# A ConvNeXt V2 block in two passes: set-up and its loads put in another order, and the GRN total placed ahead of the last expansions

## The chip, the cores and the metric

The kernel runs on one core of a Trainium2 chip. The metric is the device time in microseconds (us) of one execution. Profiles are taken by the hardware profiler in one execution of the program; times in them count from the start of the span. The engines are PE (TensorE; its weight loads are listed apart as PEld), DVE (VectorE), ACT (ScalarE), POOL (GpSimd) and SP (SyncE, which here only issues DMAs). ACT and POOL issue some DMAs too.

## The reference

```python
# x: (1, 512, 512, 96) bf16, dw: (3, 3, 96), w1: (96, 384), w2: (384, 96), gamma, beta: (384)
out = depthwise 3x3 convolution of x with dw, zero padding
h = layernorm(out) over the 96 channels            # eps 1e-5
h = gelu_tanh(h @ w1)                              # 384 channels
gx = sqrt((h * h).sum(over all pixels) + 1e-6)     # one value per channel
nx = gx / (gx.mean(over channels) + 1e-6)
h = gamma * (h * nx) + beta + h
return x + h @ w2
```

The global response normalisation (GRN) needs the sum of squares over all 262,144 pixels before any output pixel can be made.

## The kernel before

The image is cut into 128 blocks of 4 rows (2,048 pixels). There are two passes over the blocks.

The first pass is a software pipeline. A loop over slots `s` (L730) issues in each slot the steps that a table `at` has put there, for several blocks at once. For a block `b` the steps are these. `load_x` (L180) brings the block into one of four `xin` tiles, on SP. `turn_x` (L396) transposes it on DVE so that channels lie on partitions, into one of five tiles `xT`. `conv_taps` (L417) makes the depthwise convolution as 72 small matmuls with the weights `Wq`; it needs `xT` of the block and of both neighbours. In even slots without MLP work, and in all MLP slots, its result `Y` lies in one three-bank PSUM tile (pool `psY`, one buffer), in the other slots in banks of the MLP's pools. ACT copies it to `y_bf` and squares it to `ysq`. `stage_stats` sums both with matmuls into `SG`. For the first four blocks (the ramp) `stage_chain` (L518) makes the reciprocal standard deviation on DVE, and `stage_spread` (L544) spreads it by matmuls and an ACT copy to `rbc`; later blocks go by POOL and by DRAM. `stage_norm` (L589) multiplies `y_bf` by `rbc` to `yn` on POOL. `yn` goes to DRAM and comes back as `ynT` with channels on 96 partitions; the other 32 partitions of the six `ynT` tiles stay zero. `mlp_units` (L619) multiplies by the centred weight `w1p` into `U`, takes the gelu on ACT (`gsh`, `gm`), and collects the sums of squares: `bn_stats` on DVE, and a Gram matrix on PE (`gram`). A quarter of the gelu values goes to DRAM for the second pass. Block 0 has its MLP in slot 5.

Between the passes the two last blocks (`RES = 2`) are expanded anew in part (`recompute_units`, six units), two more units of the third block follow (`advance(LEAD, PRE)`), and a chain of short DVE operations makes the GRN scale: `m2`, `ssq`, three Newton steps, `gx` with its row sum `rs_`, then a PE matmul with ones (`tot_ps`), `den`, `gg`, `rden`, `sc`, the scaled weight `W2s` and the bias `B2c`.

The second pass takes the blocks in the order `ORDER`: it loads the kept quarter (`gl`), `ynT` and `x` (`xr`) five blocks ahead, recomputes the other three quarters of the gelu (`gr`), multiplies by `W2s` into `O`, and DVE adds `xb`, which is `x` plus the bias, made by POOL two blocks ahead in one of three buffers.

Every engine runs its instructions in the order in which the program issues them (class `InOrder`, L22). DMA completions are counted on a small set of semaphores that are used in turn.

The set-up stands ahead of the loop. It loads `dw`, x blocks 0 and 1, then the weights on ACT's queue, then x blocks 2 and 3. `Wq` is cleared by POOL and the zero rows of `ynT` are written by DMAs from a zero tile:

```python
pool.memset(Wq[:], 0.0)                                   # L216
for t in yn_ring:
    pool.dma_start(out=t[C:128, :, :], in_=zrow[C:128, None, :].to_broadcast([128 - C, GR, W]))
```

The tap weights `Wd` are made from `dw` by three PE matmuls and DVE, and copied into place in `Wq` by 12 copies (L363 to L370), six on DVE and six on POOL. `busy(n)` (L348) issues `n` matmuls on zeros; `FILL` gives how many, ahead of the tap weights and ahead of the loop. `setup_stats` (L372) clears `SG` and makes `rowsel`; `setup_mlp` (L378) makes `w1p` and the bias through a `psY` tile after slot 1.

Of the kernel before, what the change touches and what calls it, by code (L numbers as in the profile page):

```python
# [16 lines left out]
FILL = (6, 24)  # L17
# [36 lines left out]
def kernel(  # L54
# [105 lines left out]
    with ExitStack() as p1:  # L160
# [45 lines left out]
        for i in range(NI):  # L206
            act.dma_start(out=w1_raw[i:C:NI, :], in_=w1[chans(i), :])
        act.dma_start(out=w2_sb[:], in_=w2.rearrange("(j p) c -> p j c", p=128))
        with nc.allow_non_contiguous_dma("tiny gamma/beta load"):
            act.dma_start(out=gam_bf[:], in_=grn_gamma.rearrange("(j p) -> p j", p=128))  # L210
            act.dma_start(out=bet_bf[:], in_=grn_beta.rearrange("(j p) -> p j", p=128))
        act.activation(out=warm[:], in_=warm[:], func=ACTF.Gelu_apprx_tanh)
        for b in range(2, min(4, NBLK)):
            load_x(b)
        make_identity(nc, ident_f[:])
        pool.memset(Wq[:], 0.0)  # L216
        for t in yn_ring:
            pool.dma_start(out=t[C:128, :, :], in_=zrow[C:128, None, :].to_broadcast([128 - C, GR, W]))
# [5 lines left out]
        dve.memset(cen[:], 1.0)  # L224
# [127 lines left out]

        busy(FILL[0])
# [9 lines left out]
        for h in range(2):  # L363
            for j in range(GR):
                for q in (2 * h, 2 * h + 1):
                    a = q + GR * shift(h, j) - j + 1
                    if 0 <= a < 3:
                        n += 1
                        (dve if n % 2 else pool).tensor_copy(out=Wq[32 * q:32 * q + 32, :, :, j, :],
                                        in_=Wd[32 * q:32 * q + 32, :, 3 * a:3 * a + 3, :])  # L370

        def setup_stats():  # L372
            dve.memset(SG[:], 0.0)
            dve.memset(rowsel[:], 0.0)
            for j in range(GR):
                dve.memset(rowsel[32 * j:32 * j + 32, j:j + 1], 1.0)

        def setup_mlp():  # L378
            dve.memset(w1p[C:128, :], 0.0)
            Us = psY.tile([128, NI, W], f32, name="Y")  # L380
            w1m, b2_ps = Us[:, 0, :E], Us[:, 1, :C]
# [207 lines left out]
        def stage_norm(b):  # L589
# [3 lines left out]
            pool.tensor_tensor(out=yn[:], in0=ybf.pop(b)[:],  # L593
# [134 lines left out]
        setup_stats()  # L728
        store = None
        for s in range(last_slot + 1):  # L730
# [24 lines left out]
            def spread_out():  # L755
                for k in get("spread"):
                    stage_spread(k)
                for b in get("norma"):
                    stage_norm(b)
# [3 lines left out]
            if not mlp:  # L763
                for f in taps:
# [7 lines left out]
                if s + 2 < NBLK:  # L772
                    turn_x(s + 2)
# [57 lines left out]
            if s == 1:  # L831
# [18 lines left out]
        if store:  # L850
            store()
        for j in range(NCH):
# [4 lines left out]
        for n in range(RES):  # L857
            for f in recompute_units(ORDER[n]):
                f()
        made[0] = RES * UPB  # L860
    with p2:
        late.psU2 = p2.enter_context(tc.tile_pool(name="psU2", bufs=2, space=bass.MemoryType.PSUM))
        dve2, pe2, psO = dve, pe, late.psO
        advance(LEAD, PRE)
        gsm = p2.enter_context(tc.tile_pool(name="gsm", bufs=1))
        m2 = gsm.tile([128, NCH, NACC], f32, name="m2")
        dve2.tensor_tensor(out=m2[:], in0=mv[:, :, :, 0], in1=mv[:, :, :, 0], op=ALU.mult)
        dve2.tensor_tensor(out=m2[:], in0=m2[:], in1=mv[:, :, :, 1], op=ALU.add)
        dve2.tensor_tensor(out=m2[:], in0=m2[:], in1=npx[:, None, :].to_broadcast([128, NCH, NACC]), op=ALU.mult)
        ssq = gsm.tile([128, NCH], f32, name="ssq")  # L870
        dve2.tensor_reduce(out=ssq[:], in_=m2[:], axis=AX.X, op=ALU.add)
# [82 lines left out]
```

## Time and profile before

| | us |
|---|---|
| median of 3 runs | 1526.28 |
| range of these runs | 1525.06 to 1527.35 |
| the profiled execution | 1523.96 |
| its span in the profile | 1522.2 |
| busy in the span: ACT | 1448.8 |
| busy in the span: PE | 1424.1 |
| busy in the span: POOL | 1316.3 |
| busy in the span: DVE | 1197.0 |

The first pass takes about the first 977 us of the span, the second the rest. "Busy" counts the instructions of an engine without its register, branch, semaphore and DMA-issuing instructions. The granted clock is the share of full speed that the chip gave PE. A row of the timeline gives the start, the length, the engine, the operation with its output and inputs, how many were merged in the row, and in brackets how long the engine stood idle before it and what it waited for. "Issue" stands for a wait that the profile doesn't show.

### The profile page before, as it was taken

What the parts mean: (1) busy time and instruction counts of PE and PEld (TensorE: products, weight loads), DVE (VectorE), ACT (ScalarE), POOL (GpSimd) and SP (SyncE); (2) the same over time, 40 slices, a digit from 0 to 9 for tenths busy, and PEclk for the clock granted to TensorE, in tenths of its full rate; (3) what the DMA queues carried; (4) which work ended last, traced back from release to release, by engine and by line L of the source; (5) the groups of instructions that cost most, each with busy time, mean ns of one, the idle gap of its engine ahead of it and who ended that gap; (6) DMA issues with size and microseconds to landing.
All of it is one profiled execution on the core that took longest, in us unless ns stands there. A gap on an engine that the chain in (4) does not pass through costs nothing.

```text
span 1522.2 us, 54880 instructions
## 1 busy us (share of the span) xinstructions
PE 1424.1 (94%) x23119; PEld 816.9 (54%) x23119; DVE 1197.0 (79%) x2157; ACT 1448.8 (95%) x1692; POOL 1316.3 (86%) x933
## 2 busy tenths in 40 slices
PE   7889989999999999999999977699999999999998
PEld 2334444444444444444444443377777666666766
DVE  6749989999999999999999989755555555455555
ACT  3879999999999999999999999899999999999997
POOL 3559899999999999999999987189999999899997
PEclk8999999999999999999999999999999999999999
DMA  4668788888888788788887777789999999999996
GB/s 132 194 160 264 229 241 266 239 254 247 253 249 266 231 258 257 235 257 264 251 245 247 218 213 238 253 307 395 371 393 387 375 379 377 351 380 378 375 379 235
DMA packets 235469, 427.89 MB, mean 281 GB/s; under 512 B 34102, under 2 KB 148374, under 8 KB 235222
## 3 DMA queue, kind: packets, MB, share of 16 engines
q1 hardware_dynamic: 219972, 356.59, 72.9%
q0 software_dynamic: 13888, 67.64, 11.6%
q8 instruction: 181, 2.97, 0.8%
q14 instruction: 66, 0.54, 0.1%
q10 hardware_dynamic: 1362, 0.15, 0.1%
HBM read 272.78 MB, written 150.72 MB: 278 GB/s over the span
## 4 chain that ended last, share of the span: by engine, by line
PE 22%; POOL 18%; ACT 10%; issue 3%; DMA 2%; SPq 1%; DVE 1%; POOLq 0%; ACTq 0%
POOL xb L287 12%; PE U L32 11%; PE O L32 10%; ACT gsh L32 4%; ACT gm L32 3%; ACT y_bf L32 2%; POOL yn L32 2%; POOL ysq L32 2%; POOL xr L255 1%; SPq L32 1%; POOL gl L250 1%; PE Y L32 1%; DMA g_dram<-gsh 1%; DVE o_sb L32 1%; DMA yn_dram<-yn 1%
## 5 line engine op out<-in xcount | busy, mean ns | idle before, releaser
L32 PE MATMUL U<-ynT,w1p 128*128 128x512 bf16 x2292 | 653.5, 382 | 38.2 <-ACT gsh L32 10.6
L32 ACT ACTIVATE gr<-U 128x1536 bf16<-128x1536 f32 (+1 forms) x386 | 520.2, 1448 | 16.0 <-PE U L32 14.9
L32 DVE BATCH_NORM_STATS2 bst<-gsh 128x6 f32<-128x512 bf16 x756 | 465.7, 674 | 20.1 <-ACT gsh L32 19.5
L32 DVE TENSOR_TENSOR o_sb<-O,xb 128x384 bf16<-128x384 f32 x512 | 277.4, 556 | 252.9 <-PE O L32 148.0
L32 POOL TENSOR_TENSOR yn<-y_bf,rbc 128x1536 bf16<-128x1536 bf16 x128 | 397.4, 3107 | 81.8 <-ACT rbc L32 31.8
L287 POOL TENSOR_TENSOR xb<-xr,B2c 128x1536 f32<-128x1536 bf16 x126 | 394.7, 3134 | 37.2 <-DVE B2c L32 32.3
L32 ACT ACTIVATE gm<-U 128x512 bf16<-128x512 f32 (+1 forms) x640 | 419.4, 800 | 2.5 <-PE U L32 2.5
L32 ACT ACTIVATE gsh<-U 128x1024 bf16<-128x1024 f32 x504 | 375.4, 872 | 7.2 <-PE U L32 3.8
L32 PE MATMUL Y<-xT,Wq 64*32 64x511 bf16 (+1 forms) x8694 | 326.4, 391 | 26.4 <-ACT y_bf L32 4.8
L32 POOL TENSOR_TENSOR ysq<-y_bf 128x1536 bf16<-128x1536 bf16 x114 | 313.5, 2751 | 11.6 <-ACT y_bf L32 11.6
L32 PEld LDWEIGHTS <-w1p 128*128 128x128 bf16 x2292 | 182.7, 98 | 243.9 <-issue 157.7
L32 PEld LDWEIGHTS <-gr 128*128 128x128 bf16 x4584 | 236.3, 98 | 108.9 <-issue 24.8
L32 PE MATMUL O<-W2s,gr 128*128 128x96 bf16 x4584 | 256.6, 206 | 13.5 <-DVE o_sb L32 13.0
L32 DVE BATCH_NORM_STATS2 bst<-gm 128x6 f32<-128x512 bf16 x378 | 233.0, 672 | 0.7 <-ACT gm L32 0.7
L32 PEld LDWEIGHTS <-Wq 64*32 64x32 bf16 x9216 | 113.4, 90 | 207.9 <-issue 157.3
L32 ACT ACTIVATE y_bf<-Y 128x1536 bf16<-128x1536 f32 x121 | 187.7, 1551 | 18.2 <-PE Y L32 18.2
L32 DVE STREAM_TRANSPOSE xT<-xin 128x576 f32<-128x576 f32 (+1 forms) x256 | 181.4, 749 | 3.1 <-DMA xin<-in_x_dram 3.1
L32 PEld LDWEIGHTS <-gm 128*128 128x128 bf16 x1560 | 99.5, 98 | 85.1 <-issue 52.8
L32 PE MATMUL SG<-gm 128*128 128x128 bf16 x1560 | 130.4, 220 | 1.9 <-DVE SG L32 1.3
L32 PE MATMUL U<-w1p,ynT 128*128 128x384 bf16 (+2 forms) x780 | 126.7, 272 | 1.4 <-ACT resg L32 0.2
L255 POOL DMA_DIRECT2D xr<-in_x_dram x123 | 68.4, 556 | 35.9 <-POOL xb L287 35.9
L32 PE MATMUL O<-W2s,gl 128*128 128x96 bf16 x1512 | 84.8, 206 | 0.0
(103 smaller groups left out, 680.8 us busy)
## 6 DMA issues: line engine op xcount, KB each, us to landing
ynT<-yn_dram SPq DMA_DIRECT2D x254, 384.0 KB
xin<-in_x_dram SPq DMA_DIRECT2D x126, 432.0 KB
yn_dram<-yn SPq DMA_DIRECT2D x512, 96.0 KB
xr<-in_x_dram POOLq DMA_DIRECT2D x128, 384.0 KB, 6.6
out_dram<-o_sb SPq DMA_DIRECT2D x127, 384.0 KB
g_dram<-gsh SPq DMA_DIRECT2D x126, 384.0 KB
gl<-g_dram SPq DMA_DIRECT2D x84, 384.0 KB
gl<-g_dram POOLq DMA_DIRECT2D x42, 384.0 KB, 7.2
```

The source lines that it names most:

```text
L32: r = f(*a, **k)
L250: (pq if q % 3 == 0 else sq).dma_start(out=kept[:].rearrange("p t j w -> p (t j w)"), in_=g_dram[q])
L255: pq.dma_start(out=xr[:], in_=x[0, r0:r0 + GR].rearrange("r w c -> (r w) c").rearrange("(p g) c -> p g c", g=PXP))
L287: pq.tensor_tensor(out=xb[:], in0=grp[q]["xr"][:], in1=bias[:, None, :].to_broadcast([128, PXP, C]), op=ALU.add)
```

## The change

- x blocks 0 to 3 come first on SP. The weight loads are issued by ACT after its share of the tap copies.
- ACT clears `Wq` (one copy of zeros). The 12 tap copies go six to ACT, three to DVE, three to POOL.
- The zero rows of `ynT` are written by six POOL memsets instead of six DMAs, issued after slot 0.
- `rowsel`, `cen` and the zero rows of `w1p` are made by POOL, `SG` is cleared by DVE, all ahead of the tap weights.
- The second fill has 15 matmuls instead of 24.
- `setup_mlp` comes after slot 3 instead of slot 1 and uses one bank of the MLP's pool instead of the `psY` tile.
- `yn` of blocks 0 and 1 is made by DVE instead of POOL.
- In slots without MLP work `turn_x` is issued ahead of the convolution. On DVE's queue its place stays the same.
- The GRN chain is issued ahead of the six recomputation units instead of after all eight units; the total's matmul and what follows from it stand ahead of the sixth unit.

```diff
-FILL = (6, 24)
+FILL = (6, 15)
...
-        for i in range(NI):
-            act.dma_start(out=w1_raw[i:C:NI, :], in_=w1[chans(i), :])
-        act.dma_start(out=w2_sb[:], in_=w2.rearrange("(j p) c -> p j c", p=128))
...
         act.activation(out=warm[:], in_=warm[:], func=ACTF.Gelu_apprx_tanh)
+        act.activation(out=Wq[:].rearrange("p i d j c -> p (i d j c)").rearrange("p (a w) -> p a w", a=3),
+                       in_=zrow[:, None, :NI * GR * 32].to_broadcast([128, 3, NI * GR * 32]), func=ACTF.Identity)
         for b in range(2, min(4, NBLK)):
             load_x(b)
         make_identity(nc, ident_f[:])
-        pool.memset(Wq[:], 0.0)
-        for t in yn_ring:
-            pool.dma_start(out=t[C:128, :, :], in_=zrow[C:128, None, :].to_broadcast([128 - C, GR, W]))
...
-        dve.memset(cen[:], 1.0)
...
+        pool.memset(rowsel[:], 0.0)
+        for j in range(GR):
+            pool.memset(rowsel[32 * j:32 * j + 32, j:j + 1], 1.0)
+        pool.memset(cen[:], 1.0)
+        pool.memset(w1p[C:128, :], 0.0)
+        dve.memset(SG[:], 0.0)
         busy(FILL[0])
...
-                        (dve if n % 2 else pool).tensor_copy(out=Wq[32 * q:32 * q + 32, :, :, j, :],
-                                        in_=Wd[32 * q:32 * q + 32, :, 3 * a:3 * a + 3, :])
+                        o, i_ = Wq[32 * q:32 * q + 32, :, :, j, :], Wd[32 * q:32 * q + 32, :, 3 * a:3 * a + 3, :]
+                        if n % 2:
+                            act.activation(out=o, in_=i_, func=ACTF.Identity)
+                        elif n % 4:
+                            dve.tensor_copy(out=o, in_=i_)
+                        else:
+                            pool.tensor_copy(out=o, in_=i_)
+
+        for i in range(NI):
+            act.dma_start(out=w1_raw[i:C:NI, :], in_=w1[chans(i), :])
+        act.dma_start(out=w2_sb[:], in_=w2.rearrange("(j p) c -> p j c", p=128))
+        with nc.allow_non_contiguous_dma("tiny gamma/beta load"):
+            act.dma_start(out=gam_bf[:], in_=grn_gamma.rearrange("(j p) -> p j", p=128))
+            act.dma_start(out=bet_bf[:], in_=grn_beta.rearrange("(j p) -> p j", p=128))
+
+        def setup_ynt():
+            for t in yn_ring:
+                pool.memset(t[C:128, :, :].rearrange("p r w -> p (r w)").bitcast(f32), 0.0)
 
         def setup_mlp():
-            dve.memset(w1p[C:128, :], 0.0)
-            Us = psY.tile([128, NI, W], f32, name="Y")
-            w1m, b2_ps = Us[:, 0, :E], Us[:, 1, :C]
+            Us = banks(1)[:, 0, :]
+            w1m, b2_ps = Us[:, :E], Us[:, E:E + C]
...
-        def stage_norm(b):
+        def stage_norm(b, eng=None):
...
-            pool.tensor_tensor(out=yn[:], in0=ybf.pop(b)[:],
+            (eng or pool).tensor_tensor(out=yn[:], in0=ybf.pop(b)[:],
...
-        setup_stats()
...
-                    stage_norm(b)
+                    stage_norm(b, dve if b < 2 else pool)
...
             if not mlp:
+                if s + 2 < NBLK:
+                    turn_x(s + 2)
                 for f in taps:
                     f()
...
-                if s + 2 < NBLK:
-                    turn_x(s + 2)
...
-            if s == 1:
+            if s == 0:
+                setup_ynt()
+            if s == 3:
                 setup_mlp()
...
+        (m2, ssq, gi, three Newton steps, gx, rs_: the DVE chain, as before)
+        ahead = [f for n in range(RES) for f in recompute_units(ORDER[n])]
+        for f in ahead[:-1]:
+            f()
+        tot_ps = late.psO.tile([128, GPS, C], f32, name="O")[:, 0, 0:1]
+        pe.matmul(tot_ps, lhsT=ones_f[:], rhs=rs_[:], start=True, stop=True)
+        (den, gg, rden, sc, W2s, B2c: as before)
+        ahead[-1]()
+        made[0] = RES * UPB
+    with p2:
+        late.psU2 = p2.enter_context(tc.tile_pool(name="psU2", bufs=2, space=bass.MemoryType.PSUM))
+        advance(LEAD, PRE)
```

## The prediction

> **What bounds the kernel now.** I read the page first. Its row of the granted PE clock, in 40 slices of 38 us, is below full in the first slice alone:
>
> ```profile
> PEclk8999999999999999999999999999999999999999
> ```
>
> Next the busy time by stretches (start, end, length, busy time and count of PE, PEld, DVE, ACT, POOL, then granted clock, DMA share, GB/s):
>
> ```profile
> 0.00:43.00 43.00, 32.03 (x525) 12.31 (x525) 25.81 (x78) 16.79 (x16) 13.87 (x22) 0.84 0.51 139
> 153.00:900.00 747.00, 712.85 (x12890) 350.46 (x12889) 734.88 (x1260) 740.29 (x1051) 699.36 (x529) 1.00 0.81 246
> 980.00:990.00 10.00, 6.98 (x29) 3.38 (x29) 2.95 (x17) 6.00 (x7) 1.55 (x1) 0.60 0.27 79
> 990.00:1500.00 510.00, 497.00 (x6974) 359.78 (x6972) 264.41 (x489) 499.02 (x367) 466.32 (x282) 1.00 1.02 373
> ```
>
> From 153 to 900 us ACT works 740 of 747; after 990 ACT, PE and POOL are all over 90% busy. The change touches neither stretch. It touches the ramp (0 to 43, ACT busy 16.8 of 43) and the turn between the passes (980 to 990, PE clock 0.60). There the time is latency: one engine at a time works, the next waits for it. The waits of the ramp (total, times, longest), SP's first:
>
> ```profile
> SPq L32 <- DMA w_raw<-in_w_dram: 2.7, 1, 2.7
> ACT y_bf L32 <- PE Y L32: 9.9, 1, 9.9
> PE Y L32 <- DVE B2bc_f L32: 3.7, 1, 3.7
> DVE xT L32 <- DMA xin<-in_x_dram: 3.1, 1, 3.1
> PE U L32 <- DVE rstdx L32: 2.1, 1, 2.1
> ```
>
> SP holds block 1's load back until a weight load lands; DVE sits until block 1 lands; PE's third convolution waits until DVE has read setup_mlp's PSUM tile. The timeline (start, length, idle before):
>
> ```profile
> 11.58 1.44 DVE L32 STREAM_TRANSPOSE xT<-xin 128x576 f32<-128x576 f32 x2 [3.06 <-DMA xin<-in_x_dram]
> 16.61 1.45 ACT L32 ACTIVATE y_bf<-Y 128x1536 bf16<-128x1536 f32 x1 [9.95 <-PE Y L32]
> 24.07 4.67 PE L32 MATMUL Y<-xT,Wq 64*32 64x512 bf16 x72 [3.68 <-DVE B2bc_f L32]
> 30.07 3.13 POOL L32 TENSOR_TENSOR yn<-y_bf,rbc 128x1536 bf16<-128x1536 bf16 x1 [21.62 <-ACT rbc L32]
> 30.31 2.92 DVE L32 SCALAR_TENSOR_TENSOR var<-mom 128x16 f32<-128x16 f32 x1
> 43.65 1.51 ACT L32 ACTIVATE gsh<-U 128x1024 bf16<-128x1024 f32 x2 [0.16 <-PE U L32]
> 981.18 0.16 DVE L32 SCALAR_TENSOR_TENSOR gx<-ssq,gr 128x3 f32<-128x3 f32 x1
> 987.03 0.16 DVE L32 TENSOR_SCALAR den<-O 128x1 f32<-128x1 f32 x1 [5.68 <-PE O L32]
> 987.99 1.27 PE L32 MATMUL O<-W2s,resg 128*128 128x96 bf16 x12 [0.99 <-DVE W2s L32]
> 994.90 3.12 POOL L287 TENSOR_TENSOR xb<-xr,B2c 128x1536 f32<-128x1536 bf16 x1 [2.49 <-DVE o_sb L32]
> ```
>
> The ramp ends at 43.65, when ACT starts its first gelu and then hardly rests. A 16-column DVE step (0.17 elsewhere) lasts 2.92 and ends with POOL's yn. At the turn the sum gx is ready at 981.3, but PE takes its total only after eight units of recomputation, at 986.6.
>
> **The change, part by part: set-up.** SP: a DMA's completion semaphore is one of a few lanes in turn, and a new DMA on a lane waits for the one before it. The six transfers of blocks 0 to 3 now come ahead of the weights in that turn and leave without such a wait. Block 1 leaves near 2 us instead of 5.3. At the 260 GB/s that the traffic shows from 2 to 5 us, four blocks (1.73 MB) are in by about 8.7, block 1 near 5.5 (it was 11.5). The six zero-row DMAs (0.79 MB; 3.46 us of POOL issue) no longer compete.
>
> DVE: cen (0.17) becomes SG's memset (0.48) ahead of dwx; against it, the ident_b cast that lasted 1.05 beside POOL's Wq memset may shrink. Net 0; Wd ends at 5.3 as before. Tap copies: DVE keeps 3 of 6 (0.29 each: to 6.25), POOL 3 (0.42: to 7.2), ACT gets 6. No ACT row has 288 columns; rbc (512 columns, 0.60) and y_bf (1536, 1.45) give 0.17 + 0.83 ns a column, so 0.41 each (bounds: warm's 0.23, rbc's 0.60) and 2.5, from 5.4 to 7.9. ACT's zero fill of Wq (1152 columns, 1.1) lies ahead of Wd. PE's fill loses 9 matmuls at 0.215, ending at 8.3 instead of 10.2. DVE turns block 0 from 6.25 to 7.7 and the first half of block 1 by 8.45. So convolution 0 runs from 8.5, not 12.41, and lasts 2.9 (convolution 1's time at full clock) rather than 4.2: Y at 11.4.
>
> New wait: ACT now issues the weight loads (three w1, w2, gamma, beta: 0.37 to 0.6 each, 3.4 in all) behind its tap copies, and by the instruction order beta's waits for the lane of block 4's load. That load leaves when block 0 is turned (7.7) and lies behind blocks 0 to 3: landed at 11 to 13.5, I take 11.8. Behind it on ACT is y_bf(0): 12.2 instead of 16.6 (-4.4). The weights themselves are needed at 25.
>
> **Slots 0 to 5.** From y_bf(0): ysq done 15.15, stats 15.65, DVE's chain of 2.9 gives rstdx 18.6. setup_mlp (4 PE matmuls, 0.6; DVE 0.8) has moved to slot 3 and to another bank, so convolution 2 starts at 15.7 and, without the pause of 3.7, takes 2.9 instead of 4.67: 18.6 (was 28.7). Spread and rbc: 19.8 (was 29.9). yn(0) is now DVE's, after turn_x(4), at 20.05. Its duration is not in the trace: the o_sb row (384 columns, 0.56) scales to 1.76.
>
> The row for the port: the DVE step of 2.92 above. The Trainium skill, "SBUF — State Buffer", "Who interferes with whom", says that a DVE operation with two SBUF inputs waits out a GpSimd operation that reads SBUF. So the move to DVE also removes this 2.75 stall from chain 1, which now takes 2.9 (21.8 to 24.7) instead of 5.6. "VectorE: DVE Perf Modes", "Mode 2×_1P", would halve yn's time for packed bf16 (about 0.95), another 0.8 off at the end. I keep the row's 1.76.
>
> Then: spread(1) 25.1; rbc(1) waits behind ysq(3) on ACT, 26.6; yn(1) to 28.4; w1p, B2bc 29.2; turn_x(6) 30.6; chain 2 (3.4) 34.05. PE: stats(2) until 23.9, spread(1), setup_mlp's matmuls to 25.9, convolution 4 to 28.8; y_bf(4) frees its bank at 30.3, a burst of convolution 5, first MLP unit 31.2, gsh 31.9 (-11.8); the spread inside slot 5 waits for chain 2 at 34.1, was 44.7. **Ramp: -10.6.** yn(0), on DVE at 21.8, lands as ynT near 29.5 (7.7 us as before), before 31.2. DVE's other moved memsets (rowsel, w1p) and six ynT memsets cost POOL about 1.0 each by Wq's row (1152 columns, 1.05), at most 1.9 by bytes: done by 13.4 to 18.7, while POOL's next work, yn(2), comes near 36. turn_x moves ahead of the taps in the code but not on DVE's queue: nothing. Later work depends on these steps and on x loads that xin's slots, not bandwidth, pace, so it shifts as one.
>
> **The turn.** DVE's GRN operations keep their number; the gram sums only change places with the four that use mv. The total now stands after unit 5 of 8, where PE arrives at 981.3, as rs_ gets ready; W2s and B2c are done by 983.4 (were 988.3), and units 6 to 8 are still paced by ACT, to 986.6. Then O starts at 986.6 instead of 987.99: -1.4. POOL's xb(2) goes 5 us earlier, but xb(3) needs o_sb(0) finished (the 2.49 above: three xb buffers), and from there POOL runs nearly without rest: its xb follow each other by 4.18 on average from 994.9 to the last start at 1512.5, against 4.0 that PE needs for a block. So the second pass moves by what o_sb(0) moves.
>
> The clock: the granted clock is 0.50 from 982 to 992.1. It had also fallen to 0.50 at 12.7 after a pause of just 1.5 us (10.9 to 12.4). The skill's "TensorE: Matmul & The Clock Gate", "Part 1", asks for about 3.4 us of idleness before slowing and 3.4 of sustained work to return. By its rule PE could stay fast through all the ramp's pauses; by the row each pause of 1.5 (one remains, 29 to 30.3) may cost about 1. Its second half fits: without the 0.99 pause at 987, full speed returns about 3 us earlier, near 988.8, saving 0.7 more in block 0. **Turn: -2.1** (-1.2 to -3.3).
>
> Sum -12.7. The profiled execution took 1523.96 (span 1522.2, 1.76 around it), 2.3 under the median of 1526.28; the same difference from the median gives 1513.6.
>
> **Rivals.** A: beta's wait or the clock eats half the ramp. With all convolutions at half clock (4.4 rather than 2.9), convolutions 2 and 3 each add 1.5 to the path; block 4 landing at 13.5 adds 1.7, a slow slot 5 about 1. For it: clock 0.84 now and the ACT queue in strict order. Against it: the two long pauses are removed. Gain 5 to 9.5, with all of these 7.0: 1519.3.
> B: the ramp gain is swallowed by a rbc or ynT transfer in the sparse slots (73 to 113 us), and only the turn is left: -2, 1524. Against it: DMA share is 0.46 to 0.69 there.
> C, slower: POOL's ynT memsets hold DVE. Price: the ident_b cast (1.45 to 2.50) shows a DVE copy waiting out a POOL memset (1.36 to 2.41). The six start at 7.2; if chain 0, due at 15.7, waits for all of them, it moves to 7.2 plus six times their length. That cancels the gain of 12.7 from a length of 3.5 on, instead of 1.0; at 4.2, +4, 1530. Wq's row speaks against it.
> D: more than forecast: DVE's yn at 0.95, blocks landing early: -15 or more, 1510.5.
>
> **How the numbers follow.** Forecast 0.57 (-10 to -15), A 0.30, D 0.08, B 0.03, C 0.02. A measurement of this kernel tells about 0.2% (3.05 us) from nothing. Faster counts forecast, A, D: 0.95; B is same, C slower. The range, 1509.5 to 1519.5, takes the turn's bounds, yn's, most of A and half of D.
>
> **What would show it.** Right: DVE's second transpose pair before 9, y_bf(0) near 12, PE without a 3.7 pause at slot 2, first gsh near 32, den near 982, first O near 986.6, clock 1.00 by 989. Wrong: ACT idle before y_bf(0) on block 4's DMA past 14; 0.50 clock in 14 to 30; DVE steps of over 1 us beside POOL memsets; a rest of ACT in 73 to 113 grown by the ramp's gain; O starting at 988 or later.

## The result and the profile after

| | before | after |
|---|---|---|
| first comparison, median | 1525.67 (4 runs, 1520.56 to 1527.35) | 1507.72 (4 runs, 1506.27 to 1514.91) |
| repeated, both on one chip | 1518.75 (15 runs, 1514.98 to 1526.16) | 1509.77 (6 runs, 1505.36 to 1513.30) |
| the profiled execution | 1523.96 (span 1522.2) | 1506.65 (span 1504.8) |

All in us. The ratio was 0.9897 (95% interval 0.9857 to 0.9937) in the first comparison and 0.9934 (0.9909 to 0.9960) in the repeat. The change makes the kernel faster; how much depends on which runs are laid side by side: 18 us in the first pair of medians, 9 in the second. The first four runs of before were high for it. In 49 later runs on three chips its median was 1518.3. The forecast of 12.7 us lies between the two gains; its time of 1513.6, counted down from the high 1526.28, was too long, and the measured 1507.72 is just under its range.

The page after shows the ramp no longer below full clock in the first slice:

```profile
PEclk9999999999999999999999999999999999999999
```

The stretches (start, end, length, busy time and count of PE, PEld, DVE, ACT, POOL, then granted clock, DMA share, GB/s):

```profile
0.00:32.00 32.00, 26.75 (x543) 11.46 (x543) 22.84 (x74) 21.94 (x25) 8.46 (x23) 1.00 0.57 167
153.00:900.00 747.00, 713.15 (x12786) 350.60 (x12783) 736.16 (x1264) 742.05 (x1057) 698.89 (x530) 1.00 0.82 247
...
963.60:973.10 9.50, 6.12 (x18) 2.13 (x17) 5.01 (x32) 6.91 (x9) 3.03 (x1) 0.70 0.35 105
978.00:1490.00 512.00, 500.97 (x7026) 363.54 (x7023) 267.50 (x494) 502.03 (x370) 470.75 (x283) 1.00 1.02 373
```

The two long stretches are as before: ACT 742 of 747, then ACT, PE and POOL all over 90%. The ramp is 32 us at clock 1.00, where it was 43 at 0.84. (The record of the clock begins only at 4.79 us here, at 5.72 in the trace of before, and counts as full ahead of that; the zero matmuls of the fill start 0.43 us apart there and 0.22 behind it, so the first microseconds were slow in both.) The turn still has a clock under 1 (0.70).

The timeline after, with the rows that answer to those of before:

```profile
6.38 5.39 DVE L32 STREAM_TRANSPOSE xT<-xin 128x576 f32<-128x576 f32 x8
12.28 1.45 ACT L32 ACTIVATE y_bf<-Y 128x1536 bf16<-128x1536 f32 x1 [4.39 <-DMA gam_bf<-in_grn_gamma_dram]
15.30 0.46 PE L32 MATMUL SG<-rowsel,ysq 128*128 128x4 bf16 x12 [0.83 <-ACT ysq L32]
15.69 3.04 PE L32 MATMUL Y<-xT,Wq 64*32 64x512 bf16 x72
19.94 0.92 DVE L32 TENSOR_TENSOR yn<-y_bf,rbc 128x1536 bf16<-128x1536 bf16 x1
21.13 0.16 DVE L32 SCALAR_TENSOR_TENSOR var<-mom 128x16 f32<-128x16 f32 x1
26.53 0.96 DVE L32 TENSOR_TENSOR yn<-y_bf,rbc 128x1536 bf16<-128x1536 bf16 x1 [1.56 <-ACT rbc L32]
30.70 1.51 ACT L32 ACTIVATE gsh<-U 128x1024 bf16<-128x1024 f32 x2 [0.15 <-PE U L32]
...
967.79 0.16 DVE L32 SCALAR_TENSOR_TENSOR gx<-ssq,gr 128x3 f32<-128x3 f32 x1
968.66 0.16 DVE L32 TENSOR_SCALAR den<-O 128x1 f32<-128x1 f32 x1 [0.70 <-PE O L32]
973.12 1.16 PE L32 MATMUL O<-W2s,resg 128*128 128x96 bf16 x12
978.48 3.12 POOL L279 TENSOR_TENSOR xb<-xr,B2c 128x1536 f32<-128x1536 bf16 x1 [4.45 <-DVE o_sb L32]
```

DVE turns the first four blocks in one go, eight transposes in 5.39 us, with no wait for x. The first output is taken at 12.28 (was 16.61). Ahead of it ACT waits 4.39; the row puts that down to gamma's load, but what stands between on ACT's queue is beta's load, which waits for the semaphore (110 in the trace) that x block 4's load uses, and leaves at 11.81. The pause of 3.7 before convolution 2 is gone. The DVE step that had lasted 2.92 beside POOL's `yn` lasts 0.16. The first gelu comes at 30.70 (was 43.65). At the turn `den` follows `gx` by 0.9 instead of 5.8.

### The profile page after: what moved, and what is told of

It reads as the page before. It is cut to its first block, busy times and chain, and to the rows that moved or that the text cites. A ratio compares the mean times of both kernels' runs of the same rounds, so it can differ in the third digit from the quotient of the medians.

```text
span 1504.8 us, 54858 instructions
## 1 busy us (share of the span) xinstructions
PE 1415.3 (94%) x23110; PEld 815.8 (54%) x23110; DVE 1193.5 (79%) x2149; ACT 1450.9 (96%) x1699; POOL 1309.6 (87%) x934
## 3 DMA queue, kind: packets, MB, share of 16 engines
q0 software_dynamic: 13600, 66.86, 11.7%
## 4 chain that ended last, share of the span: by engine, by line
POOL 22%; PE 20%; ACT 12%; DVE 10%; DMA 8%; issue 3%; SPq 3%; POOLq 0%; ACTq 0%
POOL xb L279 13%; PE U L32 10%; PE O L32 9%; DVE bst L32 7%; ACT gsh L32 6%; ACT gm L32 4%; SPq L32 3%; POOL yn L32 3%; DMA ynT<-yn_dram 2%; DMA yn_dram<-yn 2%; ACT y_bf L32 2%; POOL ysq L32 2%; DMA xin<-in_x_dram 2%; DVE xT L32 2%; POOL xr L247 1%
## 5 line engine op out<-in xcount | busy, mean ns | idle before, releaser
L32 ACT ACTIVATE gr<-U 128x1536 bf16<-128x1536 f32 (+1 forms) x386 | 519.3, 1449 | 13.5 <-PE U L32 12.8
L32 POOL TENSOR_TENSOR yn<-y_bf,rbc 128x1536 bf16<-128x1536 bf16 x126 | 391.5, 3109 | 70.7 <-DMA rbc<-r_dram 26.4
L32 PE MATMUL Y<-xT,Wq 64*32 64x511 bf16 (+1 forms) x8694 | 321.7, 387 | 21.4 <-ACT y_bf L32 9.5
```

The source lines that it names most:

```text
L32: r = f(*a, **k)
```

## The experiments

The traces gave two questions. The first gelu was 12.9 us earlier and the 18th even 15.7, but the 36th only 10.3: was a part given back, and why? (These are the gelus for the sums, `gsh`; the first is number 0.) And what are set-up and turn each worth? The theory going in was that both parts work as the prediction says; the rivals are in the expectations. In what follows "the turn" is the time from the first recomputed unit (`gr`) to POOL's start of the fourth x block's `xb` (the expectations' second `xb` of the second pass). "Half clock" is a granted clock of 0.50.

**The turn's part alone.** The kernel before, with only the GRN chain moved ahead of the expansions.

```diff
-        advance(LEAD, PRE)
-        (GRN chain, tot_ps, den ... B2c)
+        (GRN chain to gx)
+        ahead = [f for n in range(RES) for f in recompute_units(ORDER[n])]
+        for f in ahead[:-1]:
+            f()
+        (tot_ps, den ... B2c)
+        ahead[-1]()
```

> The kernel before with the GRN part alone: the DVE chain ahead of the recomputation, the total's matmul ahead of the sixth unit. If the turn is worth what it seems in the two traces (first O matmul 1.3 us earlier against the first recomputed gelu, then another 1.5 from the earlier return of the PE clock), the stretch from the first recomputed gelu to the second xb of the second pass shrinks from 17.6 us to about 14.8 and the time falls by 2 to 3.5 us, to about 1523 beside 1525.7. Rival (the total was hidden behind ACT's pacing of units 6 to 8, and the gain there belongs to another clock phase): the stretch stays at 17 or more and the time stays within 1 us.

1517.62 (20 runs) against 1518.21 (23 runs): ratio 0.9995 (0.9985 to 1.0006), so -0.6 us, between -2.3 and +0.9. In its trace the turn takes 13.66 us, at full clock, against 17.63 in the first trace of before. That stretch before (columns as above)

```profile
977.26:994.90 17.64, 12.81 (x89) 7.08 (x88) 7.13 (x37) 12.51 (x13) 3.67 (x3) 0.71 0.32 90
```

and here:

```profile
977.95:991.61 13.66, 9.43 (x89) 5.40 (x88) 7.25 (x37) 12.03 (x13) 3.68 (x3) 1.00 0.41 124
```

The trace shows the step working and the time does not show it: in the trace the theory came, in the time the rival.

**The set-up alone.** The changed kernel with the old GRN tail.

```diff
-        (GRN chain ahead of the expansions, last unit behind the total)
+        for n in range(RES):
+            for f in recompute_units(ORDER[n]):
+                f()
+        advance(LEAD, PRE)
+        (GRN chain)
```

> The changed kernel with the GRN part of before: set-up, setup_mlp, yn on DVE and fill as changed. If the ramp's gain comes from there alone, the first gelu of the MLP starts near 30.7 us as in the changed kernel (43.6 before), the first recomputed gelu of the turn comes 10 to 13.6 us earlier than 977.3, the turn takes its old 17.6 us, and the time is about 1511 to 1515. Rival (the two parts need each other, for instance through the placing of tiles): first gelu later than 33, or the time above 1518.

1508.70 (4 runs), ratio 0.9941 (0.9920 to 0.9961): -9.5 us, under the 1511 to 1515 that were expected. Nearly all that the timed runs show is the set-up. First gelu at 30.77, turn 17.58 with 10.2 us of half clock.

**`yn` of blocks 0 and 1 back on POOL.**

```diff
-                    stage_norm(b, dve if b < 2 else pool)
+                    stage_norm(b, pool)
```

> The changed kernel with yn of blocks 0 and 1 on POOL again. If POOL's yn blocks a DVE step with two SBUF inputs, one step of chain 1 lasts 2 to 3 us instead of 0.17, turn_x(5) and convolution 4 come 1.5 to 2.2 us later, and the first gelu starts at 32.2 to 33 instead of 30.7. Rival (rbc(1) waits on ACT's ysq(3) anyway, so DVE had slack): no long step or one that costs nothing, first gelu within 0.5 us of 30.7.

1512.88 (one run). The timeline of this kernel:

```profile
13.69 1.45 ACT L32 ACTIVATE y_bf<-Y 128x1536 bf16<-128x1536 f32 x1 [5.80 <-DMA gam_bf<-in_grn_gamma_dram]
...
17.12 4.67 PE L32 MATMUL Y<-xT,Wq 64*32 64x512 bf16 x72
...
23.12 3.10 POOL L32 TENSOR_TENSOR yn<-y_bf,rbc 128x1536 bf16<-128x1536 bf16 x1 [10.89 <-ACT rbc L32]
23.36 2.90 DVE L32 SCALAR_TENSOR_TENSOR var<-mom 128x16 f32<-128x16 f32 x1
...
38.26 1.51 ACT L32 ACTIVATE gsh<-U 128x1024 bf16<-128x1024 f32 x2 [3.11 <-PE U L32]
```

The stall is back: DVE's step starts 0.24 behind POOL's `yn` and ends 0.04 behind its end. But the first gelu is 7.6 us later, more than a stall of 2.7 and a longer `yn` make. A part is not this edit's: the first output is taken at 13.69, and convolution 2 runs at half clock. The fair partner is the repeat of the changed kernel below, which met the same (10.2 us of half clock in the ramp, here 11.7) and had its gelu at 34.70. Against it this gelu is 3.6 later, 0.3 of it by the later first output. So the edit costs some 3 us in one pair of traces, where 1.5 to 2.3 were expected.

**`setup_mlp` back after slot 1, in the `psY` tile.**

```diff
-            Us = banks(1)[:, 0, :]
-            w1m, b2_ps = Us[:, :E], Us[:, E:E + C]
+            Us = psY.tile([128, NI, W], f32, name="Y")
+            w1m, b2_ps = Us[:, 0, :E], Us[:, 1, :C]
...
-            if s == 3:
+            if s == 1:
                 setup_mlp()
```

> The changed kernel with setup_mlp after slot 1 in the psY tile, as before. If the third convolution's wait for it was a real part of the ramp, that convolution starts near 19.5 us instead of 15.7, at half clock for part of it (4 us or more instead of 3.0), and the first gelu comes 4 to 5.5 us later, at 34.7 to 36.2. Rival (the convolution has slack, since the spread waits for DVE's chain until 18.7): the first gelu at most 1.5 us later.

1508.75 (one run). The timeline:

```profile
17.61 0.31 PE L32 MATMUL Y<-w_sb,bet_bf 128*128 128x96 bf16 x3 [1.64 <-DMA bet_bf<-in_grn_beta_dram]
19.38 4.67 PE L32 MATMUL Y<-xT,Wq 64*32 64x512 bf16 x72 [1.46 <-DVE B2bc_f L32]
...
36.62 1.51 ACT L32 ACTIVATE gsh<-U 128x1024 bf16<-128x1024 f32 x2 [1.06 <-PE U L32]
```

Convolution 2 starts 3.7 us later than 15.69, behind two waits: beta, which now comes late, and then DVE's reading of the tile. Behind these pauses it runs at half clock, and the gelu comes at 36.62, +5.9, where 4 to 5.5 were expected. The two parts of the set-up hang together: with the weights loaded late, `setup_mlp` in slot 1 holds the ramp up again. Its one timed run, at a mean clock of 0.994, shows nothing of that loss.

**The changed kernel again.**

> The changed kernel itself once more, so that the three runs beside it have it on their own chip. Theory (the ramp gives about 10 us in steady state, the turn 0.6 to 2.8): 10.5 to 13 us under the kernel before, ratio about 0.992 to 0.993. Rival (the first comparison, 0.9897, was right and the turn is worth more than the run of the turn's part alone showed): 15 us or more under it. In the trace: first gelu for the squares' sums near 30.7 us, and half-clock stretches at other places than in its first profile, since they come as windows of 3.4 us that fall where they fall.

1509.77: -9.0 us, ratio 0.9934, a little under what the theory allowed (10.5 to 13) and far from the rival's 15. Its profile is not the first one's. The timeline:

```profile
13.38 1.45 ACT L32 ACTIVATE y_bf<-Y 128x1536 bf16<-128x1536 f32 x1 [5.49 <-DMA gam_bf<-in_grn_gamma_dram]
14.89 0.46 PE L32 MATMUL SG<-rowsel,y_bf 128*128 128x4 bf16 x12 [0.83 <-ACT y_bf L32]
16.40 0.48 PE L32 MATMUL SG<-rowsel,ysq 128*128 128x4 bf16 x12 [1.06 <-ACT ysq L32]
16.81 4.67 PE L32 MATMUL Y<-xT,Wq 64*32 64x512 bf16 x72
...
34.70 1.51 ACT L32 ACTIVATE gsh<-U 128x1024 bf16<-128x1024 f32 x2 [0.18 <-PE U L32]
```

Here beta's load was let go 1.15 us later, at 12.96, and the first output was taken 1.1 later. PE then paused twice, 0.83 and 1.06 us, and from 16.0, inside the second pause, to 26.2 its clock was at half: convolution 2 takes 4.67 and the first gelu is 4.0 us later than in the first profile. My expectation that half-clock stretches "fall where they fall" was too careless: this one goes with the pauses.

**Gamma and beta loaded behind slot 0.**

```diff
-        with nc.allow_non_contiguous_dma("tiny gamma/beta load"):
-            act.dma_start(out=gam_bf[:], ...)
-            act.dma_start(out=bet_bf[:], ...)
...
             if s == 0:
                 setup_ynt()
+                with nc.allow_non_contiguous_dma("tiny gamma/beta load"):
+                    act.dma_start(out=gam_bf[:], ...)
+                    act.dma_start(out=bet_bf[:], ...)
```

> The changed kernel with the loads of GRN's gamma and beta issued behind slot 0 instead of ahead of it, so that the eviction of the first convolution's output does not stand behind them on ScalarE's queue. Theory (the wait for a DMA semaphore that x's loads hold costs the first eviction 0.8 us, and the chain of the first batch starts from that eviction): first bf16 output taken at 11.5 instead of 12.28, first gelu for sums at about 29.9 instead of 30.7; in the time under 1 us, within the spread. Rival (convolution 2 is bound by the transposes and the weights' arrival, not by that eviction): first output at 11.5, but the gelu unmoved at 30.7 within 0.3. Second rival: the loads now stand in front of the second eviction, whose wait is 1 us or more, and the gelu comes later.

The timeline:

```profile
11.76 1.45 ACT L32 ACTIVATE y_bf<-Y 128x1536 bf16<-128x1536 f32 x1 [3.86 <-PE Y L32]
...
15.16 3.05 PE L32 MATMUL Y<-xT,Wq 64*32 64x512 bf16 x72
...
30.22 1.51 ACT L32 ACTIVATE gsh<-U 128x1024 bf16<-128x1024 f32 x2 [0.16 <-PE U L32]
```

The first eviction now waits for PE alone, 0.5 us earlier, and the gelu comes 0.5 earlier: the theory's direction, at half its size. The more important thing is seen when traces are ordered by PE's pauses between convolutions 1 and 2:

| trace | beta holds the output until | PE's pauses | PE busy in the emptiest window there | half clock right behind | first gelu |
|---|---|---|---|---|---|
| gamma and beta behind slot 0 | not held (11.76) | none | 91% | none | 30.22 |
| changed kernel, first | 12.28 | 0.83 | 77% | none | 30.70 |
| fill in the turn (below) | 12.68 | 1.06 | 62% | 3.4 us | 32.12 |
| changed kernel, again | 13.38 | 0.83 and 1.06 | 54% | 10.2 us | 34.70 |
| `yn` on POOL | 13.69 | 1.15 and 1.06 | 42% | 10.2 us | 38.26 |

The other traces in which beta held the output no later than 12.28 have no half clock in this place either. So beta's wait costs 0.5 us when short, and goes with about 4 when PE loses the clock. The first row is an edit; the order of the rest is observed, in one trace each.

The fourth column says what the length of a pause does not. In each of the 14 traces all changes of the granted clock lie on one grid of 3.41 us, and where the grid lies varies between traces of one program (one of its lines is at 4.79 in the first trace of the changed kernel, at 5.75 in the second). Windows of this grid around the pauses (columns as above), in the first trace, with the fill, and in the second trace (the profile models the ends of matmuls, so the shares are rough):

```profile
11.62:15.03 3.41, 2.64 (x81) 0.92 (x60) 0.16 (x1) 2.71 (x2) 0.60 (x1) 1.00 0.96 345
...
12.78:16.19 3.41, 2.10 (x72) 1.12 (x64) 0.00 (x0) 3.38 (x3) 0.00 (x0) 1.00 0.74 257
16.19:19.61 3.42, 3.22 (x56) 0.83 (x59) 2.97 (x14) 2.34 (x3) 0.00 (x0) 0.50 0.02 5
...
12.57:15.99 3.42, 1.84 (x60) 0.65 (x36) 0.00 (x0) 2.58 (x2) 0.00 (x0) 1.00 0.94 349
15.99:19.40 3.41, 2.88 (x60) 1.04 (x60) 2.04 (x13) 3.24 (x4) 0.00 (x0) 0.50 0.06 13
```

PE is busy 2.64, 2.10 and 1.84 us of a window, and behind the second and third the clock is 0.50. Over the 14 traces, of 38 windows at full clock in which PE was busy under 41%, 37 were followed by one at half clock; of 130 with 41 to 65%, 31; of 5,903 with more, none. The longest pause in a window tells less: from 1.06 to 1.5 us 24 of 61 were followed by half clock, from 1.5 to 2 us 8 of 22. The 0.83 us of the first trace (14.47 to 15.30) lay across a line of the grid, at 15.03. Since the lines fall elsewhere in the next execution of the same program, whether a given pause costs the clock is in part chance.
In the timed runs nothing can be told from this edit: 1510.46 (6 runs), ratio 0.9933 (0.9904 to 0.9963), the same as the changed kernel's.

**The weight loads ahead of ScalarE's work.** Only ACT's queue changes.

```diff
         for b in range(min(2, NBLK)):
             load_x(b)
+        (w1, w2, gamma and beta loads by ACT)
         act.activation(out=warm[:], in_=warm[:], func=ACTF.Gelu_apprx_tanh)
...
-        (the same loads behind the tap copies)
```

> The changed kernel with the loads of w, W2, gamma and beta put back on ScalarE's queue ahead of the warm-up gelu and of the clearing of Wq. Theory (eight DMA issues of 0.4 to 0.6 us each stand ahead of ScalarE's part of the tap weights, and nothing else moves): the clearing of Wq starts 3.5 to 4.5 us later, the tap copies end at 11.5 to 12.5 instead of 7.9, conv 0 ends and its output is taken at 15 to 16.5 instead of 12.28, and the first gelu for sums comes 3 to 4 us later, at 33.7 to 34.7. Rival (ScalarE's queue has slack there, x's loads alone matter): first output at 12.3 to 13.3, gelu within 1 us of 30.7; the wait for gamma's semaphore, 0.8 us, is gone.

1508.50 (one run). The timeline of ACT:

```profile
5.01 1.28 ACT L32 ACT_TABLE_LOAD   x1 [5.01 <-DMA xin<-in_x_dram]
...
6.44 1.15 ACT L32 ACTIVATE Wq<-zrow 128x1152 bf16<-128x1152 bf16 x1
7.62 2.47 ACT L32 ACTIVATE Wq<-Wd 32x288 bf16<-32x288 bf16 x6
13.70 1.45 ACT L32 ACTIVATE y_bf<-Y 128x1536 bf16<-128x1536 f32 x1 [3.60 <-PE Y L32]
```

ACT's clearing starts 3.6 us later (6.44 against 2.82), its tap copies end at 10.1 against 7.9. The first output comes 1.4 later, though beta, which leaves at 4.53 here, no longer holds it, and the gelu, at 33.29, 2.6 later. Expected were 3 to 4: the direction is the theory's, the size between it and the rival.

**Tap copies on two engines.**

```diff
                         if n % 2:
-                            act.activation(out=o, in_=i_, func=ACTF.Identity)
-                        elif n % 4:
                             dve.tensor_copy(out=o, in_=i_)
```

> The changed kernel with its tap-weight copies on two engines, VectorE and GpSimd, instead of three: ScalarE's six go to VectorE (3 to 9 copies of 0.31). Theory (conv 0 waits for its transposes, which VectorE does behind the copies, so each copy that VectorE gets back is paid in full): transposes start 1.9 us later, conv 0's first wait ends at 9.5 to 10.5 instead of 8.5, the first output is taken at 13.5 to 14.2, the first gelu 1.5 to 2 us later. Rival (conv 0 is bound by the fill of 15 matmuls, 4.04 to 7.8, and the output by gamma's semaphore at 11.8): first output within 0.4 us of 12.28.

The edit does less to DVE than the expectation says: it leaves six copies to DVE and six to POOL, not nine and three.

```profile
5.42 1.64 DVE L32 COPY Wq<-Wd 32x288 bf16<-32x288 bf16 x6
7.09 5.39 DVE L32 STREAM_TRANSPOSE xT<-xin 128x576 f32<-128x576 f32 x8
...
12.11 1.45 ACT L32 ACTIVATE y_bf<-Y 128x1536 bf16<-128x1536 f32 x1 [8.15 <-PE Y L32]
```

The transposes begin 0.71 us later (7.09 against 6.38), and so does convolution 0 behind its first six matmuls (9.24 against 8.53): up to there DVE's three further copies are paid in full. But the first output comes at 12.11 and the first gelu at 30.78; 1509.94 (one run). That is the rival's number for another reason than the rival's: ACT, without copies, issues its loads earlier, beta at 6.67, and the held output (12.28) becomes one that waits for PE. So in this order of the loads ScalarE's share in the copies is worth nothing. Where beta does not hold the output anyway (gamma and beta behind slot 0: 11.76 and 30.22) the three engines come 0.35 us earlier at the output and 0.56 at the gelu, by one trace each.

**Squares of outputs 17 and 18 on ACT.** The given-back part. The waits of the changed kernel between 90 and 135 us have these lines:

```profile
PE SG L32 <- POOL ysq L32: 4.1, 1, 4.1
...
ACT gm L32 <- PE U L32: 3.0, 1, 3.0
```

```diff
-                stage_sq(b, False)
+                stage_sq(b, b in (17, 18))
```

> The changed kernel with the squares of convolution outputs 17 and 18 on ScalarE instead of GpSimd. Theory (the 16 us that the changed kernel was ahead near 100 us fell to 10.2 because TensorE, ahead of GpSimd, had to wait 4.1 us for GpSimd's square of output 17, and lost the clock right behind that wait): the wait goes, the shift against before at the 36th gelu for sums is 12 us or more instead of 10.2, and the time falls by 1 to 2 us against the changed kernel. Rival (GpSimd's row of multiplications and squares is only the last in a line, ScalarE is just as late there): ScalarE takes 1.5 to 3 us more, the 36th gelu comes no earlier, and the time is within 1 us of the changed kernel's.

The sums of that square in the timeline of the changed kernel:

```profile
115.99 0.48 PE L32 MATMUL SG<-rowsel,ysq 128*128 128x4 bf16 x12 [4.10 <-POOL ysq L32]
```

and in that of the edited one, where they run without a wait:

```profile
113.64 0.44 PE L32 MATMUL SG<-rowsel,ysq 128*128 128x4 bf16 x12
```

No half clock follows; in the changed kernel it lay from 114.0, inside the wait, to 120.8. The 36th gelu comes at 130.22, against 134.11 and 137.97 in the two traces of the changed kernel: the shift against the first trace of before (144.38) is 14.2 where 12 or more was expected. In the time it is 1506.37 (8 runs), ratio 0.9920 (0.9896 to 0.9943), which overlaps the changed kernel's 0.9934.

**Zero multiplications in the turn.** `fill(n)` issues n matmuls of zeros, 128x384, into an `O` tile. The 7 stand behind the third unit, not behind the fourth as the expectation says.

```diff
         for n, f in enumerate(ahead[:-1]):
             f()
+            if n == 2:
+                fill(7)
...
+        fill(6)
```

> The changed kernel with 13 multiplications by zeros, into a tile of the output's kind that nothing reads, set into the turn: 7 behind the fourth of the units computed ahead, 6 behind the last, ahead of the scale's part. Theory (the turn's remaining length is TensorE standing idle and then running at half clock): the granted clock stays at 1.00 through the turn, the stretch from the first recomputed unit to the first output multiplication falls from 9.5 to about 7.5 to 8 us, and the one to the fourth x block's residual from 14.8 to about 13; the time falls by 1 to 2 us. Rival (half-clock windows come by themselves, whether or not TensorE is idle): the clock drops as before in some runs, and the fill adds up to 1 us; time within 1 us either way.

The turn takes 13.65 at full clock; 1504.90 (4 runs), ratio 0.9906 (0.9877 to 0.9935). The first output multiplication comes 7.86 behind the first unit, as expected. But the repeat of the changed kernel has 13.65 and 7.86 too, without fill, having met no half clock there. So the fill shortens nothing by itself. Without it, 4 of 9 traces with the new tail had a full clock in the turn; with it, 2 of 2 had, which is too few to show that the fill keeps it full.

**The kernel before again.**

> The kernel before once more, for its trace. Open is why the turn's part alone takes 3 to 4 us off the turn in the traces (17.6 us from the first recomputed unit to the residual of the fourth x block in the two traces with the old order, 13.65 to 14.8 in those with the new) and only 0.6 us off the timed median. Theory A (the new order is worth over 2 us in the turn, and the timed runs lose it elsewhere): the turn takes 15.5 us or more here even if the clock is full in it, and 17.6 with 10.2 us of half clock. Theory B (both traces with the old order happened to meet a half-clock window of 10.2 us, and the order itself is worth 1 us or less): with a full clock the turn takes 14.6 us or less. Whatever the clock, the first gelu for sums comes at 40 to 44 us, 10 or more behind the changed kernel's 30.7.

1517.21. The timeline:

```profile
40.93 1.51 ACT L32 ACTIVATE gsh<-U 128x1024 bf16<-128x1024 f32 x2 [0.16 <-PE U L32]
...
981.13 0.16 DVE L32 TENSOR_SCALAR den<-O 128x1 f32<-128x1 f32 x1 [5.70 <-PE O L32]
...
982.09 1.27 PE L32 MATMUL O<-W2s,resg 128*128 128x96 bf16 x12 [0.99 <-DVE W2s L32]
...
988.52 3.12 POOL L287 TENSOR_TENSOR xb<-xr,B2c 128x1536 f32<-128x1536 bf16 x1 [2.01 <-DVE o_sb L32]
```

The turn is 17.15 us, again with 10.2 us of half clock: all three traces with the old tail have that. It never ran at full clock, so what the expectation would have read from a full clock could not be read. But three of three speaks against theory B, by which the two earlier ones were hit by chance.

**Both low ones together.** Squares 17 and 18 on ACT and the fill.

```diff
-                stage_sq(b, False)
+                stage_sq(b, b in (17, 18))
...
+                fill(7)
...
+        fill(6)
```

> The changed kernel with both edits that had the lowest medians together: squares of outputs 17 and 18 on ScalarE (1506.37 alone) and the 13 multiplications by zeros in the turn (1504.90 alone), against 1509.77 for the changed kernel beside them. Theory A (each is worth 1 to 3 us by itself): 1502 to 1504, some 6 us under the changed kernel. Theory B (at an equal mean clock they were worth nothing, only their runs had a higher clock, 0.995 against 0.992): 1505 to 1508 with the mean clock at 0.993 to 0.995, and a time that follows the clock by about 1.15 us for each 0.001.

1502.59 (6 runs, 1500.35 to 1503.45), against 1517.41 for before on its chip: ratio 0.9891 (0.9867 to 0.9914), 14.8 us. This is faster than before, and than the changed kernel by 7 us between medians from different chips (where before had 1517.41 and 1518.75); the intervals against before, 0.9867 to 0.9914 and 0.9909 to 0.9960, overlap only between 0.9909 and 0.9914. Gamma and beta behind slot 0 as well, which by the table above takes the other cause out of the ramp, was not run with these. The stretches of this trace:

```profile
0.00:32.00 32.00, 27.54 (x543) 11.98 (x543) 22.97 (x74) 21.80 (x25) 8.46 (x23) 1.00 0.55 167
112.00:122.00 10.00, 9.75 (x168) 4.91 (x167) 10.00 (x18) 10.00 (x16) 10.00 (x4) 1.00 0.77 236
955.00:974.00 19.00, 16.27 (x154) 10.24 (x154) 12.47 (x43) 16.38 (x22) 3.67 (x2) 1.00 0.57 199
```

The clock is 1.00 in all three critical places (in the first, from the start of its record at 7.11 on). Theory A's time came, by theory B's mechanism: the mean clock of the six runs is 0.998, where the changed kernel's ten had 0.989 to 0.994.

That the clock carries the spread can be shown over all runs. One line through the 112 timed runs that have a clock, with a level for each kernel and one common slope, gives 1.17 us for each 0.001 of mean clock, and leaves 1.7 us of scatter (root mean square). At a clock of 0.993 the levels are 1516.5 for before, 1515.9 for the turn's part, 1508.1 for the set-up's, 1507.1 and 1508.3 for the changed kernel, 1510.4 with gamma and beta late, 1509.6, 1508.6 and 1507.9 for the last three edits (squares, fill, both). At an equal clock the last three are no faster than the changed kernel; what they gain goes with the clock. (It has two levels for the changed kernel, one for each set of its runs.) The line is a description: the kernel sets part of its own clock, the clock is rounded to 0.001, and the runs of both edits, at 0.996 to 1.000, lie outside the 0.989 to 0.994 of the changed kernel, so that 1507.9 is read off beyond them. That the two edits raised the clock is shown for the squares by the wait that is gone from their place; for the fill it is not shown.

## Why the prediction was right, and where it was not

**Set-up, right nearly to the step.** Forecast and first trace: transposes begin 6.25 and 6.38; tap copies end 7.9 and 7.9; convolution 0 starts at 8.5 and 8.53 (its first six matmuls at 7.86); beta's load leaves at 11.8 and 11.81; first output taken 12.2 and 12.28; convolution 2 starts at 15.7 and 15.69; `yn(0)` 20.05 and 19.94; first gelu 31.9 and 30.70. That beta's load agrees to 0.01 is luck: in the eight traces in which it waits for block 4's load it left between 11.51 and 13.27, and what holds is the range that I gave for that load, 11 to 13.5. Not every part that I costed earns anything: the three-engine split of the copies is worth nothing as long as beta stands behind them. Of the signs that I named for being wrong one came, not in the first trace but in the repeat: half clock between 14 and 30 us.

**The mis-sized term: `yn` on DVE.** I kept the scaled row, 1.76, against the Trainium skill's "VectorE: DVE Perf Modes", "Mode 2×_1P", whose halving gives about 0.95, an estimate. The rows show 0.92 and 0.96. The row I scaled, `o_sb`, has f32 inputs; `yn` has only bf16. It should have been scaled by type as well as by size. This accounts for 0.8 of the 1.2 by which the gelu came earlier than forecast.

**The port, right.** The Trainium skill, "SBUF — State Buffer", "Who interferes with whom", and the row of 2.92 agreed on the stall; with `yn` on POOL it was 2.90 again, without it 0.16. Rival C did not come: POOL's `ynT` memsets took 0.95 each (forecast 1.0), and DVE's eight transposes beside them followed each other every 0.67, without a wait.

**The ramp's sum, right on average, with a part in it that comes and goes.** Forecast -10.6. The mean over the traces with the old set-up (43.65, 40.93, 41.98) is 42.19; over those of the changed kernel, the set-up alone, and the edits of squares, fill and both (30.70, 34.70, 30.77, 30.85, 32.12, 30.85) it is 31.67. That is -10.5 at the first gelu, and the 36th moves by -10.7 where squares stay on POOL (145.18 to 134.49; means of three traces, and of six: the changed kernel twice, the set-up alone, fill, gamma and beta late, two-engine taps). But of this some 3 us are clock. The old ramp had 6.8, 10.2 and 13.6 us of half clock in its three traces (40.93, 41.98, 43.65), the new one 10.2, 3.4 and none (34.70, 32.12, 30.70; the other three next to none): both grow by about 0.4 for each us of half clock and lie some 7.5 apart, 7.3 where the length is the same. The forecast had the same two parts in it: convolutions 0 and 2 at 2.9 instead of 4.2 and 4.67 are 3.1 of its 10.6. What it left out is that the new ramp does not always keep its clock. Rival A weighed "the clock eats half" at 0.30, and in the repeat it ate 4.0; over the six traces it ate 1 on average, so the agreement of -10.5 with -10.6 owes something to which executions were traced.

**What was given back.** It only looked so. From the 18th to the 36th gelu the changed kernel took 39.49 us and the first trace of before 34.07, but before's second trace took 38.97, and the turn's part alone 39.17: in the first trace of before the half clock had come already at 104.7, ahead of that stretch. A wait for POOL's square is in both kernels (3.0 us in the second trace of before, 4.1 in the changed kernel). This was rival B's region, and its mechanism, a transfer, had no share in it.

**The clock rule: less idleness suffices than the page says, and pauses are the wrong thing to count.** The Trainium skill, "TensorE: Matmul & The Clock Gate", "Part 1", wants about 3.4 us of idleness before slowing. A window of about that length is in the traces, as the grid of 3.41 us, but it need not be idle throughout: PE was busy 62%, 54% and 42% in the three windows of the table behind which the ramp lost its clock. My row, read as a pause of 1.5 us (it says 1.74), gave the right direction. As a rule of pauses it does not hold: pauses of 0.83 and 1.06 went with a loss, one of 1.46 in the second trace of before (10.65 to 12.11, PE busy 56% of its window) did not.

**The turn, right in the traces, missing in the times.** Forecast -2.1 (-1.2 to -3.3). The first pair has 17.63 and 14.82: -2.8. Over three old and nine new tails without fill the means are 17.45 and 14.19: -3.3. `den` came 0.9 behind `gx`, as the order said. The first O came 9.5 behind the first recomputed unit (forecast 9.3). The forecast that the clock would be full 3 us earlier came true in the first trace, 6.8 us of half clock instead of 10.2; over the nine it was 3.0 on average, none in four. With none the turn takes 13.65, with 3.4 about 14.3, with 6.8 about 14.8; continued to 10.2 that is about 15.4 where the old tail took 17.15 to 17.63. So of the 3.3 some 2 us are the order and the rest is clock, by this estimate. In the timed runs the turn's part gave 0.6 (-0.9 to 2.3), and the changed kernel is no faster than the set-up alone. I can't reconcile the two fully. It is not lost behind the turn: from there to the end all traces take 526.2 to 527.3. Ahead of it the traces scatter by more than the gain: from the 36th to the 486th gelu they take 787.1 to 792.7, old tail or new. At most a small part returns just ahead of the turn: from the 486th gelu to the first recomputed unit the old tail's traces take 39.8 to 41.7 (mean 41.1), the new one's 39.8 to 43.4 (mean 41.5), and four of the latter nine, and one of the former three, have half clock there. The mean clock of the turn's part alone, 0.9913, is that of before, 0.9910, though its turn met none in its trace; so its timed runs must have met as much half clock as those of before, in the turn or elsewhere. Where, the timed runs can't show. This stays open.

**The base.** The sum of -12.7 was taken from 1526.28, a median of three. Before's own later runs, 1518.3, are 8 us lower. The first profile had a mean clock of 0.988; by the slope above that is 3.5 us against the 0.991 of the later runs, a part of the 8. I had taken the base as good to 0.2%, 3.05 us. Against the pooled gain (median 1508.75 of the ten runs of the changed kernel, 1518.3 for before: -9.6) the sum of -12.7 is 3 too much, and about half of that is what the turn fails to show (-0.6 for -2.1).

## What to carry to other kernels

Price a short wait of TensorE by what stands behind it: in the ramp an eviction held 1.1 us longer came with a first gelu 4.0 us later, because the clock fell. Look for the load that stands ahead of an eviction on the same queue, and move it behind; here the trace showed that gain (0.5 us at the first gelu) and the timed runs did not. And before a gain is read from two traces, take a second trace of the kernel before and compare stretches with the same length of half clock.

## What the runs showed of the hardware that I had not expected

- The granted clock changes on a grid of 3.41 us, and where it lies varies between executions of one program. It fell behind 37 of 38 windows in which TensorE was busy under 41%, behind 31 of 130 with 41 to 65%, and behind none of 5,903 with more. A window of 54%, with a pause of 0.83 us and the beginning of one of 1.06, was followed by 10.2 us at half clock, and the convolution in it took 4.67 instead of 3.04.
- The run-to-run spread of the changed kernel, 1505.4 to 1514.9 in ten runs, follows the mean granted clock at 1.17 us for each 0.001. The one with both edits spread less, 1500.35 to 1503.45 in six.
- A load's wait for a completion semaphore that another queue's load holds differs from execution to execution: beta left at 11.51 to 13.27 in traces of nearly the same program.
